# A two-network kernel after linear attention: the first network's first chunk in two halves, with the second chunk between them

## The chip, the cores and the metric

The kernel runs on one core of one Trainium2 chip. The metric is the device time of one execution, in microseconds (us). The core has five engines, each with a queue of its own that runs in order: TensorE (PE in the profile; its weight loads are PEld), VectorE (DVE), ScalarE (ACT), GpSimd (POOL) and SyncE (SP, used here for DMA issues). Sixteen DMA engines move data between DRAM and the on-chip memory SBUF; TensorE writes to PSUM, eight banks of 128 x 512 fp32.

## The reference

```python
def _attn_ref(q, k, v, alpha):            # 4 x 8 heads, 768 steps, head size 48
    for t in range(S):
        state = alpha[:, :, t, :, None] * state + np.einsum('bhd,bhe->bhde', k[:, :, t], v[:, :, t])
        y[:, :, t] = np.einsum('bhd,bhde->bhe', q[:, :, t], state)
def _moe_ref(x, w_in, w_out):             # 3072 tokens, 384 -> 2048 -> 384
    h = x @ w_in
    g = np.where(h > 0.0, h, np.exp(np.minimum(h, 0.0)) - 1.0)
    return g @ w_out
def _moe2_ref(x, domain_probs, w1, w2):   # 4 experts, 384 -> 1024 -> 384
    p = domain_probs / (domain_probs.sum(-1, keepdims=True) + 1e-09)
    for e in range(E):
        out += p[:, e:e + 1] * (np.maximum(x @ w1[e], 0.0) @ w2[e])
```

The output is the second network applied to the first network applied to the attention, for all 3072 tokens.

## The kernel before

The 768 steps are cut into six chunks of 128 (`NCH`). One chunk of all four batches is 4 x 128 = 512 tokens, the free size of every large matmul. A unit is one chunk of one batch; 24 units of attention run in order, and the state of a batch is carried from chunk to chunk.

The first network works chunk by chunk. Its 2048 hidden features are 16 slices of 128 (`F1`). For each slice `first` multiplies the chunk's input with the slice's part of w_in (`g1`, nine matmuls: three blocks of 128 inputs, and three products each because every fp32 number is split into a high and a low part), takes the ELU (`elu`: two operations on ScalarE, one on VectorE, and the split, one on each) and `second` multiplies with the slice's part of w_out (`g2a`, nine matmuls), which adds up over the slices in three PSUM banks t0, t1 and t2 (`self.xa`). The list `items` holds all pairs of chunk and slice, 96 of them; `second` runs `LA` = 2 items behind `first`. After a chunk's last slice `end1` copies the three banks to a staging tile ("stg", two buffers) on ScalarE and writes it to DRAM (`x1d`), where the second network picks it up.

The weights of the first network come as float64. `load_f64` brings one slice into a staging tile, `conv_f64` makes fp32 of it and splits it: two ScalarE and four VectorE operations (lines 71 to 78 and 327 to 328). Slice 0 is converted ahead of the loop, slice 1 is under way, and the others follow one an item, a few items ahead of their use in chunk 0. From then on all slices stay in SBUF.

The attention of chunk c + 1 runs between the items of chunk c. `unit_steps` gives six steps a unit: scores and transposes (`scores`, `ktrans`), three steps of preparation of the next unit (`prep0`, `prep1`, `prep2`), outputs and state (`yout_t`, `state`), and `xtrans`, which splits the unit's output into the chunk's input `x0`, a tile with the tag X0 or X1 by turns (`c % 2`). `yout_t` copies the output from PSUM into the one buffer "y", writes it to DRAM (`x0d`, two issues on ScalarE's queue), and reads it back in the layout that the network needs (tile `xr`, in the same buffer "y"). `slots` spreads the 24 steps of a chunk evenly over the 28 half-items of the first 14 slices (a half-item lies behind `first` or behind `second`); after every sixth step a unit of raw attention input is loaded.

`post` holds further work by item: the conversions, the preparation of the second network's weights (`prep_w`, items 20 to 91), and in the last chunk the inputs of the second network (`prep_x0`, from item 80 on). The second network follows from some 558 us on; its tiles reuse X0 and X1 (inputs' sums `xs` and weights `wa` in X0, hidden values `g` in X1).

Within the loop over the items no order is written out by hand. A planner, part of the framework, gives each engine its order when the program is built: what comes earlier in the program goes first, as soon as the planner's own costs say that its inputs and its buffer are there. On the chip each engine then keeps that order and waits where an input is late.

## Time and profile before

| | us |
|---|---|
| median of three runs | 1294.45 |
| lowest and highest | 1293.82, 1300.0 |
| the profiled execution | 1298.41 |
| its span, first to last instruction | 1296.6 |
| TensorE busy in the span | 1252.3 (97%) |
| VectorE busy | 876.4 (68%) |
| ScalarE busy | 579.5 (45%) |
| GpSimd busy | 518.5 (40%) |

The span falls into the attention of chunk 0 (0 to 42.6 us), the six chunks of the first network (first matmul of each at 42.6, 135.5, 219.3, 305.7, 391.7 and 471.9 us) and the second network, whose first matmuls begin among the last of chunk 5 at some 551 us. A busy share is a mean over stages: TensorE's 97% says that little of the whole is lost, and it is a view by stage that says where.

### The profile page before, as it was taken

To read this page: it belongs to the slowest core of one execution; us is meant where nothing else is said; L and a number is where in the kernel's file an instruction comes from. 1 tells how busy PE (TensorE), PEld (TensorE's weight loads), DVE (VectorE), ACT (ScalarE), POOL (GpSimd) and SP (SyncE) were. 2 spreads that over 40 slices of the span, in tenths; PEclk is the share of its full clock that TensorE was granted. 3 is DMA by queue.
4 is the path that set the end of the run, shared out by engine and by line. 5 is a ranking of instruction groups with operands and counts; after the bars stand their busy time and mean duration, and the time that the engine had idled before them with its cause. 6 is when DMAs were issued, how large, how long until landed. Compare 5 with 4: busy or idle time off the path is not lost.

```text
span 1296.6 us, 17731 instructions
## 1 busy us (share of the span) xinstructions
PE 1252.3 (97%) x6457; PEld 1013.4 (78%) x6457; DVE 876.4 (68%) x1510; ACT 579.5 (45%) x1076; POOL 518.5 (40%) x405
## 2 busy tenths in 40 slices
PE   8999999999999987999999999899999999999997
PEld 6776787877777876878878888788888878888886
DVE  8899977786877632366756666566767576757664
ACT  5666756665666645434333242334332333233241
POOL 0000000000000046068777564887956465456562
PEclk8999999999999998999999999999999999999999
DMA  6545266766575631525747358765644574435232
GB/s 243 199 167 183 103 233 211 253 204 226 214 255 178 227 105 50 218 89 216 254 153 270 109 190 321 273 234 200 245 184 163 211 294 171 173 105 205 98 114 72
DMA packets 71535, 246.70 MB, mean 190 GB/s; under 512 B 6680, under 2 KB 38264, under 8 KB 62096
## 3 DMA queue, kind: packets, MB, share of 16 engines
q1 hardware_dynamic: 68016, 236.84, 51.4%
q10 hardware_dynamic: 3424, 8.65, 1.7%
q8 instruction: 53, 0.87, 0.3%
q14 instruction: 42, 0.34, 0.1%
HBM read 182.11 MB, written 63.36 MB: 189 GB/s over the span
## 4 chain that ended last, share of the span: by engine, by line
PE 68%; DMA 10%; DVE 10%; POOL 4%; ACT 4%; issue 3%; SPq 1%; ACTq 0%; DVEq 0%; POOLq 0%
PE h L648 22%; PE t L698 13%; PE a L698 9%; PE h L366 7%; PE t L389 7%; PE h L698 4%; DMA x0d<-yt 3%; DMA raw<-in_att_dram 2%; DMA wraw<-in_we_dram 2%; DMA xr<-x0d 1%; DVE wh L328 1%; DVE u L668 1%; DVE h L379 1%; DVE g L328 1%; PE a L267 1%
## 5 line engine op out<-in xcount | busy, mean ns | idle before, releaser
L668 DVE TENSOR_TENSOR u<-h,u 128x512 f32<-128x512 f32 x258 | 177.4, 688 | 89.1 <-PE h L648 87.9
L389 PE MATMUL t<-g,w_W 128*128 128x512 f32 x864 | 220.3, 396 | 16.0 <-ACT x1raw L850 10.8
L366 PE MATMUL h<-x,w_W 128*128 128x512 f32 x864 | 218.5, 395 | 7.8 <-DVE g L328 5.6
L648 PE MATMUL h<-xc_Q,wa 128*128 128x512 f32 x780 | 219.3, 391 | 3.5 <-DVE c L668 2.4
L628 POOL TENSOR_TENSOR g_W<-c,g_W 128x512 fp32r<-128x512 f32 x128 | 164.4, 1299 | 122.0 <-ACT c L627 103.8
L389 PEld LDWEIGHTS t<-g,w_W 128*128 128x128 f32 x864 | 161.4, 189 | 53.9 <-ACT x1raw L850 11.2
L626 ACT ACTIVATE g_W<-c 128x512 fp32r<-128x512 f32 x128 | 80.0, 626 | 272.2 <-DVE c L668 158.8
L493 POOL TENSOR_TENSOR xs<-xr 128x512 f32<-128x512 f32 x8 | 10.1, 1274 | 471.0 <-DMA xr<-x1d 471.0
L366 PEld LDWEIGHTS h<-x,w_W 128*128 128x128 f32 x864 | 160.3, 189 | 45.6 <-DVE g L328 7.3
L648 PEld LDWEIGHTS h<-xc_Q,wa 128*128 128x128 f32 x780 | 145.7, 188 | 36.5 <-DVE c L668 3.7
L698 PE MATMUL t<-g_W,wb 128*128 128x512 f32 x576 | 157.6, 389 | 0.0
L698 PEld LDWEIGHTS t<-g_W,wb 128*128 128x128 f32 x576 | 108.1, 188 | 22.6 <-POOL g_W L628 0.2
L627 ACT ACTIVATE c<-c 128x512 f32<-128x512 f32 x192 | 121.0, 632 | 7.4
L668 DVE TENSOR_TENSOR c<-u,h 128x512 f32<-128x512 f32 x123 | 84.0, 685 | 50.2 <-PE h L648 37.8
L648 PE MATMUL h<-xc_W,wa 128*128 128x512 f32 x390 | 110.2, 391 | 4.6 <-DVE u L668 2.6
L662 DVE COPY u<-h 128x512 f32<-128x512 f32 x99 | 68.1, 690 | 66.8 <-PE h L648 66.5
L698 PE MATMUL a<-g_W,wb 128*128 128x512 f32 x384 | 111.8, 390 | 0.6 <-POOL g_W L628 0.6
L628 POOL TENSOR_TENSOR g_X<-c,g_X 128x512 fp32r<-128x512 f32 x64 | 82.7, 1304 | 62.6 <-ACT c L627 51.7
L379 DVE SCALAR_TENSOR_TENSOR h<-e,h 128x512 f32<-128x512 f32 x96 | 66.3, 690 | 56.4 <-ACT e L378 56.2
L626 ACT ACTIVATE g_X<-c 128x512 fp32r<-128x512 f32 x64 | 40.0, 626 | 141.7 <-DVE c L668 78.5
L648 PEld LDWEIGHTS h<-xc_W,wa 128*128 128x128 f32 x390 | 72.7, 188 | 22.2 <-DVE u L668 4.0
L328 DVE TENSOR_TENSOR g<-h,g 128x512 fp32r<-128x512 f32 x96 | 65.9, 687 | 30.5 <-ACT g L327 30.2
(138 smaller groups left out, 1935.7 us busy)
## 6 DMA issues: line engine op xcount, KB each, us to landing
wa<-wad SPq DMA_DIRECT2D x33, 1536.0 KB, 6.7
wb<-wbd SPq DMA_DIRECT2D x30, 1536.0 KB, 6.6
raw<-in_att_dram SPq DMA_DIRECT2D x22, 960.0 KB, 6.4
wad<-wh SPq DMA_DIRECT2D x44, 384.0 KB, 2.5
wbd<-wh SPq DMA_DIRECT2D x43, 384.0 KB, 3.3
xcd<-xh SPq DMA_DIRECT2D x30, 512.0 KB, 3.0
wraw<-in_wm_dram SPq DMA_DIRECT2D x16, 768.0 KB, 4.3
wraw<-in_we_dram SPq DMA_DIRECT2D x20, 576.0 KB, 5.4
```

Of the source, the lines that this page charges most:

```text
L267: nc.tensor.matmul(ps[64 * j:64 * j + 64, a * C:(a + 1) * C], self.st[b][r, a, :], raw[r, Q0 + a * C:Q0 + (a + 1) * C], start=(a == 0), st ...
L328: (eng or nc.vector).tensor_tensor(out=lo, in0=src, in1=hi.bitcast(F32), op=ALU.subtract)
L366: nc.tensor.matmul(h[:, 0:n], w[:, wl, fi, k * 128:(k + 1) * 128], x[:, xl, k, n0:n0 + n], start=(k == 0 and i == 0), stop=(k == KD - 1 an ...
L379: nc.vector.scalar_tensor_tensor(out=h, in0=e, scalar=-1.0, in1=h, op0=ALU.add, op1=ALU.max)
L389: nc.tensor.matmul(self.xa[k][:, 0:n], w[:, wl, fi, DM + k * 128:DM + (k + 1) * 128], g[:, gl, 0:n], start=(f == 0 and i == 0), stop=(f == ...
L626: nc.scalar.activation(out=g[:, n, 0], in_=v, func=AF.Relu)
L627: nc.scalar.activation(out=v, in_=v, func=AF.Relu)
L628: nc.gpsimd.tensor_tensor(out=g[:, n, 1], in0=v, in1=g[:, n, 0].bitcast(F32), op=ALU.subtract)
L648: nc.tensor.matmul(b, w[:, wl], x[:, xl], start=(j == 0), stop=(j == 2))
L662: nc.vector.tensor_copy(out, b)
L668: (nc.vector if "b" in (a0, a1) or dst == "S5" else nc.gpsimd).tensor_tensor(out=out, in0=val(a0, b), in1=val(a1, b), op=ALU.add if op == ...
L698: nc.tensor.matmul(oa[m, d], wt[:, f, wl, d * 128:(d + 1) * 128], G[m][:, f, gl], start=first, stop=last)
```

## The change

The list of items gets a new order: chunk 0's slices 0 to 7, chunk 1's 16 slices, chunk 0's slices 8 to 15, and then chunks 2 to 5 as before. At the end of chunk 0's first half the three banks are copied out as at the end of a chunk and written to a new DRAM tile `x1p`; they are read back into a staging tile at item 28, and at the end of the second half VectorE adds them to the banks, in place of ScalarE's copies.

Chunk 1's attention then has its 24 steps in the twelve half-items of the first six items. Chunk 2's attention has one step in each of items 19 to 23 and the rest in items 23 to 29, since its input uses the tag X1, which chunk 1 reads until item 23. The conversions of slices 8 and 9 stand at items 6 and 8, those of slices 10 to 15 at items 12 to 17, two items behind their loads; slices 3 to 7 stay where they were. The tags of the inputs follow the new order (`XTAG`), and in the second network X0 and X1 change places. The computation is the same but for the order in which the two halves of chunk 0's sums are added.

```diff
--- before.py
+++ after.py
@@ -25,6 +25,8 @@
 Q0, K0, A0, V0 = 0, NP * C, 2 * NP * C, 3 * NP * C
 UW = V0 + DM
 LA = 2
+FS = 8
+XTAG = (0, 1, 1, 0, 1, 0)
 SW = 64 + D
 REBASE = 2.0 ** -112
 P_LO, P_SUM = 1e-16, 1e15
@@ -88,6 +90,7 @@
         self.ok = ok
         self.att, self.wm, self.we, self.probs, self.out = att, wm, we, probs, out
         self.x0d = [dram.tile([2 * D, NP * C], F32, name=f"x0d{b}") for b in range(B)]
+        self.x1p = dram.tile([128, KD, 512], F32, name="x1p")
         self.x1d = [dram.tile([128, KD, 512], F32, name=f"x1d{c}") for c in range(NCH)]
         self.wad = [dram.tile([128, 12, 2, 128], F32, name=f"wad{g}") for g in range(NG)]
         self.wbd = [dram.tile([128, 3072], F32, name=f"wbd{g}") for g in range(NG)]
@@ -311,7 +314,7 @@
         c, b = u
         y = self.y.pop(u)
         if c not in self.x0:
-            self.x0[c] = self.big.tile([128, 2, KD, 512], F32R, tag=f"X{c % 2}", name=f"x0_{c % 2}")
+            self.x0[c] = self.big.tile([128, 2, KD, 512], F32R, tag=f"X{XTAG[c]}", name=f"x0_{XTAG[c]}")
         x0 = self.x0[c]
         if c:
             v = y
@@ -380,15 +383,15 @@
         self.split(g[:, 0, 0:n], g[:, 1, 0:n], h)
         return g
 
-    def g2a(self, w, fi, g, n, f):
-        nc = self.nc
-        if f == 0:
+    def g2a(self, w, fi, g, n, first, last):
+        nc = self.nc
+        if first:
             self.xa = [self.bank(f"t{k}") for k in range(KD)]
         for k in range(KD):
             for i, (wl, gl) in enumerate(((0, 0), (0, 1), (1, 0))):
                 nc.tensor.matmul(
                     self.xa[k][:, 0:n], w[:, wl, fi, DM + k * 128:DM + (k + 1) * 128], g[:, gl, 0:n],
-                    start=(f == 0 and i == 0), stop=(f == F1 - 1 and i == 2),
+                    start=(first and i == 0), stop=(last and i == 2),
                 )
 
 
@@ -507,7 +510,7 @@
                     )
                 x[m, k] = t
 
-        tmp = self.big.tile([128, 6, 512], F32, tag="X0", name="xs")
+        tmp = self.big.tile([128, 6, 512], F32, tag="X1", name="xs")
         sn, v = [0], {}
 
         def base(p):
@@ -596,7 +599,7 @@
         self.xc.setdefault(r, []).append(t)
 
     def load_wa(self, i):
-        t = self.big.tile([128, 12, 2, 128], F32R, tag=("W2", "X0")[i % 2], name="wa")
+        t = self.big.tile([128, 12, 2, 128], F32R, tag=("W2", "X1")[i % 2], name="wa")
         self.nc.sync.dma_start(out=t.bitcast(F32), in_=self.wad[i % NG])
         self.wa[i] = t
 
@@ -650,7 +653,7 @@
                 if isinstance(dst, tuple):
                     m, f = dst
                     if m not in G:
-                        t = ("W6", "X1", "W7")[self.gn % 3]
+                        t = ("W6", "X0", "W7")[self.gn % 3]
                         self.gn += 1
                         G[m] = self.big.tile([128, 3, 2, 512], F32R, tag=t, name=f"g_{t}")
                     out = self.ctile()
@@ -793,18 +796,29 @@
         self.ab = ("a0", "a1")
         pe_order.__exit__(None, None, None)
 
-        blocks = [(c, (0, 1, 2, 3)) for c in range(NCH)]
-        per = [units[4 * c + 4:4 * c + 8] for c in range(NCH)]
-        items = [(bi, f) for bi in range(len(blocks)) for f in range(F1)]
+
+
+        parts = [(0, 0, FS), (1, 0, F1), (0, FS, F1)] + [(c, 0, F1) for c in range(2, NCH)]
+        items = [(c, f, a, b) for c, a, b in parts for f in range(a, b)]
         n1 = len(items)
+        half = lambda a, b: [(i, k) for i in range(a, b) for k in range(2)]
         slots = {}
-        for bi, us in enumerate(per):
-            steps = [s for u in us for s in seq[units.index(u)]]
-            av = [(bi * F1 + f, k) for f in range(F1 - LA) for k in range(2)]
+        for c in range(1, NCH):
+            steps = [s for u in units[4 * c:4 * c + 4] for s in seq[units.index(u)]]
+            if c == 1:
+                av = half(0, FS - LA)
+            elif c == 2:
+                av = half(F1 + FS - 1, 2 * F1 - LA)
+            else:
+                av = half(F1 * (c - 1), F1 * c - LA)
             for n, s in enumerate(steps):
-                slots.setdefault(av[n * len(av) // len(steps)], []).append(s)
+                if c == 2:
+                    k = (F1 + FS - 5 + n, 0) if n < 5 else av[(n - 5) * len(av) // (len(steps) - 5)]
+                else:
+                    k = av[n * len(av) // len(steps)]
+                slots.setdefault(k, []).append(s)
                 if n % 6 == 5:
-                    slots[av[n * len(av) // len(steps)]].append([(load_next, ())])
+                    slots[k].append([(load_next, ())])
 
         def open_p2():
             self.attn.__exit__(None, None, None)
@@ -813,10 +827,13 @@
 
         post = {}
         at = lambda i, f, *a: post.setdefault(i, []).append((f, a))
-        for f in range(nf, F1):
+        for f in range(nf, FS):
             at(f - nf, self.conv_f64, f)
+            at(f - nf, self.load_f64, f + 2)
+        for f in range(FS, F1):
+            at((FS - 2, FS)[f - FS] if f < FS + 2 else f + 2, self.conv_f64, f)
             if f + 2 < F1:
-                at(f - nf, self.load_f64, f + 2)
+                at(f + 2, self.load_f64, f + 2)
         b5 = n1 - F1
         at(b5 - 2, open_p2)
         at(F1 + 1, self.norm_probs)
@@ -838,24 +855,34 @@
         gs = {}
 
         def first(it):
-            bi, f = it
-            c, bs = blocks[bi]
-            n = 128 * len(bs)
-            h = self.g1(self.w1[f // 2], f % 2, self.x0[c], bs[0] * 128, n)
-            gs[it] = self.elu(h, n)
-
-        def end1(c):
-            t = self.stg.tile([128, KD, 512], F32, tag="stg", name="x1raw")
+            c, f = it[:2]
+            h = self.g1(self.w1[f // 2], f % 2, self.x0[c], 0, 512)
+            gs[it] = self.elu(h, 512)
+
+        part = []
+
+        def load_part():
+            t = self.stg.tile([128, KD, 512], F32, tag="stg", name="x1part")
+            nc.sync.dma_start(out=t, in_=self.x1p)
+            part.append(t)
+
+        at(2 * F1 - 4, load_part)
+
+        def end1(c, a, b):
+            t = part.pop() if a else self.stg.tile([128, KD, 512], F32, tag="stg", name="x1raw")
             for k in range(KD):
-                nc.scalar.copy(t[:, k], self.xa[k])
-            nc.scalar.dma_start(out=self.x1d[c], in_=t)
+                if a:
+                    nc.vector.tensor_tensor(out=t[:, k], in0=self.xa[k], in1=t[:, k], op=ALU.add)
+                else:
+                    nc.scalar.copy(t[:, k], self.xa[k])
+            nc.scalar.dma_start(out=self.x1d[c] if b == F1 else self.x1p, in_=t)
 
         def second(it):
             g = gs.pop(it)
-            bi, f = it
-            self.g2a(self.w1[f // 2], f % 2, g, 512, f)
-            if f == F1 - 1:
-                end1(bi)
+            c, f, a, b = it
+            self.g2a(self.w1[f // 2], f % 2, g, 512, f == a, f == b - 1)
+            if f == b - 1:
+                end1(c, a, b)
 
         for i in range(n1):
             first(items[i])
```

## Rows read from the trace of the kernel before

**Rows 1.** The page: VectorE's busy tenths in 40 slices of the span.
```profile
DVE  8899977786877632366756666566767576757664
```

**Rows 2.** Busy time by stretch: first matmul of chunks 0, 1, 2 and 3.
```profile
core 0: us, PE busy (x) PEld busy (x) DVE busy (x) ACT busy (x) POOL busy (x), PEclk, DMA share, GB/s
42.60:135.50 92.90, 86.34 (x559) 66.34 (x559) 88.64 (x145) 60.59 (x105) 0.00 (x0) 1.00 0.52 179
135.50:219.30 83.80, 82.20 (x545) 66.88 (x545) 68.62 (x153) 53.72 (x119) 0.00 (x0) 1.00 0.57 198
219.30:305.70 86.40, 83.91 (x561) 67.75 (x560) 66.18 (x144) 53.36 (x118) 0.00 (x0) 1.00 0.64 221
```

**Rows 3.** TensorE's waits, whole span: who waited for what: us, times, longest.
```profile
PE t L389 <- ACT x1raw L850: 10.8, 1, 10.8
...
PE t L389 <- ACT g L327: 2.8, 4, 1.3
...
PE h L366 <- ACT w_W L327: 2.2, 3, 1.2
```

**Rows 4.** Timeline of TensorE in chunk 1: start, length, instructions merged.
```profile
144.34 1.09 PE L267 MATMUL a<-raw,st 48*64 48x128 f32 x16
...
146.82 2.34 PE L366 MATMUL h<-x,w_W 128*128 128x512 f32 x9
149.00 2.20 PE L389 MATMUL t<-g,w_W 128*128 128x512 f32 x9
151.04 2.20 PE L366 MATMUL h<-x,w_W 128*128 128x512 f32 x9
...
155.22 1.16 PE L218 MATMUL a<-raw 48*128 48x128 f32 x16
...
156.72 2.32 PE L366 MATMUL h<-x,w_W 128*128 128x512 f32 x9
```

**Rows 5.** VectorE's groups, 42.6 to 135.5 us: count | busy us, mean ns | idle.
```profile
L328 DVE TENSOR_TENSOR w_W<-cv,w_W 128x768 fp32r<-128x768 f32 x15 | 14.3, 954 | 2.0 <-ACT w_W L327 1.9
L75 DVE SCALAR_TENSOR_TENSOR cv<-wraw,cv 128x768 int32<-128x768 int32 x14 | 13.3, 950 | 0.0
...
L379 DVE SCALAR_TENSOR_TENSOR h<-e,h 128x512 f32<-128x512 f32 x15 | 10.3, 688 | 0.7 <-ACT e L378 0.7
L328 DVE TENSOR_TENSOR g<-h,g 128x512 fp32r<-128x512 f32 x15 | 10.2, 683 | 1.4 <-ACT g L327 1.4
L72 DVE TENSOR_SCALAR cv<-cv 128x768 int32<-128x768 int32 x14 | 7.6, 546 | 0.0
L181 DVE TENSOR_TENSOR_SCAN P<-raw,plo 128x128 f32<-128x128 f32 x19 | 6.5, 402 | 0.0
L224 DVE TENSOR_TENSOR sm<-a,mask 128x512 f32<-128x512 f32 x10 | 6.5, 680 | 0.0
```

**Rows 6.** Timelines of ScalarE and VectorE: copies into "y", splits out of it.
```profile
52.65 0.57 ACT L279 COPY yt<-a 112x512 f32<-112x512 f32 x1
75.86 0.58 ACT L279 COPY yt<-a 112x512 f32<-112x512 f32 x1
...
62.60 0.54 DVE L328 TENSOR_TENSOR x<-xr,x 128x384 fp32r<-128x384 f32 x1
87.96 0.55 DVE L328 TENSOR_TENSOR x<-xr,x 128x384 fp32r<-128x384 f32 x1
```

**Rows 7.** DMA issues of the page: count, KB each, median us to landing.
```profile
x1d<-x1raw ACTq DMA_DIRECT2D x6, 768.0 KB, 3.9
```

**Rows 8.** Timeline of ScalarE and TensorE at chunk 4's end, idle before in brackets.
```profile
491.37 0.62 ACT L327 CAST xc_Q<-xs 128x512 fp32r<-128x512 f32 x1 [6.23 <-POOL xs L493]
...
493.02 4.21 PE L389 MATMUL t<-g,w_W 128*128 128x512 f32 x9 [10.76 <-ACT x1raw L850]
497.02 2.98 PE L366 MATMUL h<-x,w_W 128*128 128x512 f32 x9
499.84 2.20 PE L389 MATMUL t<-g,w_W 128*128 128x512 f32 x9
```

## The prediction

> **What bounds the kernel now.** I read three views in this order. First the page: the span is the table's 1296.6 us, and the row of tenths of VectorE shows nines only in the slices that lie between some 65 and 162 us [rows 1]. Then the busy time by stretch, cut at the first matmul of each chunk of the first network: in chunk 0's stretch, 42.6 to 135.5 us, VectorE is busy 88.64 of 92.90 us (95%), in chunk 1's 68.62 of 83.80 (82%), in chunk 2's 66.18 of 86.40 (77%) [rows 2]. So TensorE sets the pace nearly everywhere, and VectorE only in chunk 0. Then TensorE's waits there: the named ones are short; 2.8 and 2.2 us are for ScalarE's casts of the hidden layer and of the weights, all of them in that stretch, and those casts themselves follow VectorE's work [rows 3].
>
> How much chunk 0 loses: one group of nine matmuls (a slice's first or second layer) takes 2.04 us from start to start (149.00 to 151.04); a unit of attention takes TensorE 144.34 to 146.82 = 2.48 us for its outputs and state and 155.22 to 156.72 = 1.50 us for scores and transposes, and the group after each part 2.18 for 2.04, so some 4.2 us [rows 4]. The stretch of chunk 0 holds 16 first and, because the second layer runs two slices late, 14 second groups, four units and the scores of a fifth: 30 x 2.04 + 4 x 4.2 + 1.1 = 79.1 us. It took 92.9, so 13.8 us are lost. Chunk 1 by the same count needs 32 x 2.04 + 16.8 - 1.1 = 81.0 and took 83.8 (2.8 lost), chunk 2 needs 82.1 and took 86.4 (4.3 lost) [rows 2]. 13.8 us is the most that a change to chunk 0 alone can win, 1.1% of the time.
>
> Why VectorE is full there: 14 conversions of weights, each 0.950 + 0.948 (a second such operation) + 0.546 + 0.954 = 3.40 us by mean durations [rows 5], lie beside the four units and the ELUs. The groups of that view add up to 98.4 us against 88.64 busy, since each operation starts a little before the one ahead ends: what follows is multiplied by 0.90.
>
> **The change, part by part.** I call the three new parts A (chunk 0, slices 0 to 7, items 0 to 7), B (chunk 1, items 8 to 23) and C (chunk 0, slices 8 to 15, items 24 to 31); from item 32 on the order is the old one.
>
> Moved: the conversions of slices 8 to 15, 8 x 3.40 x 0.90 = 24.5 us of VectorE, go out of the first 93 us and stand beside B's 65.3 us of matmuls. B's VectorE work is then 24.5 + 16 ELUs x 1.37 x 0.90 = 19.7, and some 10 for the probabilities, the first second-network weights and the first steps of chunk 2: 54 of 65 us. I cost B at nothing; the cover is those 11 us, and if it were gone it would cost what chunk 1 loses now, 2.8.
>
> Squeezed: the four units of chunk 1 have twelve half-slices instead of 28. Two things set when item 8, which needs all four, can begin.
> VectorE: the last step of one conversion and six whole ones 21.3 us, the units 26.6 (scans 5.5, masks 5.2, four 128x512 operations a unit, at the ELU's 0.68, 10.9, splits 2.2, states 2.8), eight ELUs 11.0; together 58.9 x 0.90 = 53.0 us. Chunk 2's first preparation and the last two ELUs (6.1) are not needed for item 8. At the 95% seen now that is 49.4 to 55.8 us after 42.6: item 8 at 92.0 to 98.4 [rows 2, 5].
> The one buffer "y": a unit's output is copied into it, goes to DRAM, comes back into it and is split, and only then may the next unit's copy start. From the copy's start to the end of the split it now takes 52.65 to 63.1 = 10.5 us for the first unit and 75.86 to 88.5 = 12.6 for the slowest; four units lie between 10.4 and 12.6, 11.1 in the mean [rows 6]. The first copy can stand at 49 (an estimate: its step comes a slice sooner) to 52.65, so the fourth split ends at 94 to 97.5. I take 97.5, the later ends of both.
>
> TensorE's work that can run before item 8 is eight first and eight second groups and four units: 16 x 2.04 + 16.8 = 49.4 us, until 92.0. So a wait of 5.5 us is left in A. In TensorE's queue the last two second groups may stand behind item 8's first group (they do in the order of the program; the planner may draw them ahead): 4.1 us or nothing, I take 2. A loses 7.5 where chunk 0 lost 13.8: minus 6.3. The bounds: minus 12.8 (a wait of 1 us) and plus 4.5 (the chain at 12.6 a unit, item 8 at 103.5, 11.5 us after 92.0, both groups behind it, 4.1, and the lower clock of below, 2.7: 18.3 for 13.8).
>
> C: chunk 2's first unit waits in "y" with its split until item 23 has read chunk 1's input (both use X1); what is queued behind that split is ScalarE's ELU work of the same item, which needs the same matmuls, so nobody waits longer. Three units follow in the buffer, 3 x 11.1 = 33 us, while TensorE has 8 items and three units, 45 us: a margin of 12. VectorE in that stretch: 19 of 24 steps of the units 19, eight ELUs 9.9, weights of the second network at chunk 2's rate (66.18 less units 23.9 and ELUs 19.7, so 22.6 over 16 slices) 11.3, three additions 1.9: 42 of 45 to 47 us, 90%. That lies between chunk 1's 82% (2.8 us lost) and chunk 0's 95% (13.8 lost in twice the length): 1 to 6, less the share that this half loses now (1.4). I take plus 1.5, nearest to chunk 1's row, with bounds 0 and 4.5.
>
> Added: one more end of a part, three ScalarE copies like those that now end a chunk and one issue on ScalarE's queue; at all chunk ends but one nobody waits for such copies, the next part's first group covers them [rows 3]. It writes 768 KB, as the write of a chunk does, 3.9 us to landing [rows 7]. The sums come back by one load on SyncE's queue at item 28, five items (over 20 us) before their use, into a staging buffer that is free by then; what stands behind it in that queue is loads that are as early. Cost nothing, and 3.9 us once if it had no cover. At the end of C three VectorE additions replace three copies: a 128x512 operation on a PSUM operand is 0.69 [rows 5], the group of 2.04 us ahead of the next part covers the first, and VectorE's queue is 90% full there: 0 to 2.5 us, I take 0.5.
>
> The swap of X0 and X1 in the second network changes no dependency that I can find. The long wait at 482 to 493 us, where chunk 4's end stands in ScalarE's queue behind casts that wait for GpSimd [rows 8], lies far from the change; I leave it as it is.
>
> Sum: -6.3 + 1.5 + 0.5 = -4.3. On the profiled execution's 1298.4 that is 1294.1; that execution is 4 us above the median of the runs, 1294.45, and from the median it is **1290.1**.
>
> One row speaks against a single long wait in place of many short ones. After the wait of 10.76 us the next nine matmuls took 493.02 to 497.02 = 4.00 us, half rate, the 1.2 GHz level, and the nine after them 2.82: 2.7 us more than two groups cost [rows 8]; the many short waits of chunk 0 left the granted clock at 1.00 [rows 2]. The Trainium skill, "TensorE: Matmul & The Clock Gate", section "HAM oscillation — how this bites in real kernels", says that an idle gap that is long enough puts the array back to half rate, and that the way back up is then paid again after every such gap; the trace agrees at 482 us. By that rule the wait before item 8 would cost 2.7 more and the sum would be -1.6; without it, as put down, -4.3.
>
> **The rivals.**
> Slower: the pitch of the units. If the chain through "y" takes 14 us a unit because copy, split and masks now queue on a VectorE that is fuller still, item 8 starts at 53.1 + 4 x 14 = 109.1 (53.1 is 97.5 less 4 x 11.1), 17.1 us after TensorE has run dry; with the clock's 2.7 and the 2 of the order A loses 21.8 against 13.8, and with C the time is 1294.45 + 8 + 2 = 1304. It decides from 12.2 us a unit upward (item 8 at 101.8, a loss of 11.8, the gain eaten by A, C and the additions). For it: one of four chains took 12.6, and the scores of a unit now stand over 20 us ahead of its split. Against it: three of four took 10.4 to 11.1 on a VectorE that was 95% busy.
> Nothing won: the wait comes back whole in front of item 8, or half there and half in C; 1294 to 1297. For it: A has nearly as much VectorE work per matmul as chunk 0 had (53.0 to 49.4 us).
> More won: the planner draws all eight second groups ahead and item 8 starts by 95 us: A loses 1 to 3, and with C and the additions at 0 to 2 the time is 1281.6 to 1286; or the long wait at 482 us falls away too when the planner orders ScalarE anew, 13 us more, some 1277. Against it: both limits of A lie behind 92.0.
>
> **How the numbers follow.** The forecast (1.5 to 8 us won) 0.50, nothing won 0.17, slower 0.18, more won 0.15. Half a per cent, about what a measurement of this kernel can tell from no change, is 6.5 us: faster by more has the 0.15 and some 0.20 of the forecast's 0.50; slower by more has 0.12 of the rival's 0.18; the rest is within. The range leaves out the late wait's end and the rival's far end: 1281 to 1299.5.
>
> **What would show it.** The first group of item 8 at 95 to 100 us, with one wait of 3 to 8 us ahead of it; copies into "y" 10 to 12 us apart between 50 and 90; VectorE over 95% busy until then and under 85% in B; B's 16 items in 66 to 68 us; the start of item 32 at most 3 us late; the wait at chunk 4's end unchanged. The second network starts some 4 us sooner than 558.3 and takes as long as before. Wrong it would be if the units come 13 us or more apart, if the wait ahead of item 8 passes 10 us, or if the late wait moves.

## The result and the profile after

The changed kernel takes 1314.19 us (median of four runs, 1313.34 to 1314.4); the kernel before, run beside it, 1297.22. The ratio of the runs is 1.0124 with a 95% interval of 1.0079 to 1.0169 (the intervals below are of the same kind, each against the kernel before run beside it): some 16 us slower, where 4 us less had been forecast, and outside the range. The profiled execution of after has a span of 1312.6 us for 1296.6. Cut at the first matmul of the same items, the 16.0 us between the two spans lie here:

| stretch, by items | before, us | after, us | difference |
|---|---|---|---|
| start to item 0 | 42.6 | 40.9 | -1.7 |
| 0 to 15 (after: A and half of B) | 92.9 | 95.0 | +2.1 |
| 16 to 31 (after: the rest of B, then C) | 83.8 | 83.7 | -0.1 |
| 32 to 47 (chunk 2) | 86.4 | 92.3 | +5.9 |
| 48 to 63 (chunk 3) | 86.0 | 88.5 | +2.5 |
| 64 to 79 (chunk 4) | 80.2 | 81.2 | +1.0 |
| 80 to the second network (chunk 5) | 78.9 | 82.3 | +3.4 |
| second network | 745.8 | 748.7 | +2.9 |

The gain that was forecast for the first row of items is a small loss, and most of the loss lies behind item 32, where the order of the items is the old one. From the page of after, VectorE's tenths, a digit for 32.8 us:

```profile
span 1312.6 us, 17739 instructions
DVE  8889978777777742366756665566667575757664
```

Two nines for the three of before [rows 1], and they lie from 98 to 164 us, nearly all in B: in A, where VectorE was to be fuller than ever, stand eights. The busy times by stretch say it in numbers: A, B and C alone, then the stretches of 16 items that answer to [rows 2]. Columns: the stretch and its length, busy time with instructions of PE, PEld, DVE, ACT and POOL, the granted clock, the DMA share, GB/s.

```profile
40.90:104.50 63.60, 57.26 (x418) 43.18 (x417) 55.19 (x96) 38.15 (x70) 0.00 (x0) 0.95 0.55 187
104.50:174.00 69.50, 69.47 (x357) 56.78 (x358) 60.62 (x107) 46.49 (x86) 0.00 (x0) 1.00 0.38 127
174.00:219.60 45.60, 44.62 (x329) 35.91 (x327) 36.27 (x79) 28.17 (x63) 0.00 (x0) 1.00 0.73 258
...
40.90:135.90 95.00, 88.62 (x556) 68.85 (x555) 84.65 (x144) 62.86 (x115) 0.00 (x0) 0.96 0.50 168
135.90:219.60 83.70, 82.72 (x549) 67.02 (x547) 67.43 (x138) 49.95 (x103) 0.00 (x0) 1.00 0.57 198
219.60:311.90 92.30, 86.15 (x560) 69.04 (x561) 68.66 (x150) 53.97 (x117) 0.00 (x0) 0.98 0.62 213
```

In A VectorE's work is 55.19 us, 2 more than the sum of the prediction, but it takes 63.6 us to do it: 87% busy, not 95. In B TensorE is busy 69.47 of 69.50 us and waits for nobody, as forecast; the 69.5 us are over the 66 to 68 that were named as a sign, and VectorE's 60.62 us (87%) over the 54 and the 85%. Why A is slow stands in these lines of the timeline of after, from the split of its first unit to the copy of its third:

```profile
58.82 0.56 DVE L331 TENSOR_TENSOR x<-xr,x 128x384 fp32r<-128x384 f32 x1 [1.85 <-ACT x L330]
59.91 1.28 DVE L227 TENSOR_TENSOR sm<-a,mask 128x512 f32<-128x512 f32 x2
65.53 0.59 ACT L282 COPY yt<-a 112x512 f32<-112x512 f32 x1 [0.31 <-PE a L277]
77.15 0.56 DVE L331 TENSOR_TENSOR x<-xr,x 128x384 fp32r<-128x384 f32 x1 [1.37 <-ACT x L330]
78.22 0.68 DVE L227 TENSOR_TENSOR sm<-a,mask 128x512 f32<-128x512 f32 x1
79.94 0.96 PE L277 MATMUL a<-sm,raw 128*48 128x128 f32 x13
81.05 0.59 ACT L282 COPY yt<-a 112x512 f32<-112x512 f32 x1 [2.06 <-PE a L277]
```

Read it as one chain. VectorE's queue is in order, and in it the mask of the next unit's scores stands directly behind the split of this one (both masks behind the first split, the second of two behind the second). The split waits for the round trip of "y" through DRAM, VectorE idles for it (1.85, 1.37 us), and only then come the mask, TensorE's outputs of the next unit and their copy into "y". So the parts that [rows 6] show far apart in the kernel before are in series: copy to the end of the split takes 9.9, 12.2, 10.5 and 10.7 us, in the prediction's bounds of 10.4 to 12.6 or just below, but from the end of a split to the next copy pass another 6.1, 3.4 and 2.8. (In the 6.1 TensorE ran at half rate, as shown below: the unit's two groups of 16 matmuls took 1.97 and 1.95 us, in the fourth unit 1.09 and 1.08.) The copies stand at 49.47, 65.53, 81.05 and 94.43, 15.0 us apart in the mean. Item 8 starts at 104.5, and the loss does not stand ahead of it as one wait. Two of TensorE's waits in A, at 59 and 87 us, and the one at item 8:

```profile
59.33 0.77 PE L392 MATMUL t<-g,w_W 128*128 128x512 f32 x2 [1.97 <-ACT g L330]
...
87.68 0.66 PE L238 MATMUL h<-ident,raw 128*128 128x128 f32 x4 [1.96 <-DVE raw L203]
...
104.53 0.73 PE L369 MATMUL h<-x,w_W 128*128 128x512 f32 x2 [0.49 <-ACT x L330]
```

The clock fell too. Granted clock (0.50 is the 1.2 GHz level) in two stretches of after, the first of them right behind the wait at 59 us, and then around the wait at 87 us:

```profile
59.90:66.70 6.80, 6.80 (x53) 5.46 (x53) 6.56 (x13) 4.21 (x9) 0.00 (x0) 0.50 0.03 14
247.60:251.00 3.40, 3.40 (x10) 2.66 (x9) 2.85 (x6) 2.70 (x7) 0.00 (x0) 0.50 0.97 335
```

```profile
84.00:92.00 8.00, 5.90 (x35) 3.60 (x33) 8.00 (x16) 7.08 (x13) 0.00 (x0) 1.00 0.67 244
```

A third such stretch of 3.4 us lies at 582 us, behind a wait of 2.17 us. None of the three is in the trace of before. TensorE is busy all through them, so they cost at most half of 13.6 us, 6.8 of the 16; in the first, VectorE is busy 6.56 of the 6.80 us too, so what it cost is not shown. The wait of 1.96 us at 87.68 left the clock at 1.00: the length of the single wait does not decide.

In chunk 2's stretch the loss is in the first eight items (50.1 us where before took 43.2; the other eight are 1.0 shorter). Its largest wait, in the timeline of after:

```profile
234.26 0.95 SPq L174 DMA_DIRECT2D raw<-in_att_dram  x1
...
243.67 0.42 DVE L184 TENSOR_TENSOR_SCAN P<-raw,plo 128x128 f32<-128x128 f32 x1 [3.11 <-DMA raw<-in_att_dram]
...
246.48 0.68 DVE L331 TENSOR_TENSOR g<-h,g 128x512 fp32r<-128x512 f32 x1
247.21 3.04 PE L369 MATMUL h<-x,w_W 128*128 128x512 f32 x7 [3.72 <-DVE g L331]
```

A load of a unit's input lands 9.4 us after its issue; VectorE stands 3.11 us at the scan that needs it; an ELU's split stands behind that scan, and TensorE waits 3.72 us for the split. Last, the long wait at chunk 4's end, beside [rows 8]:

```profile
505.58 0.62 ACT L330 CAST xc_Q<-xs 128x512 fp32r<-128x512 f32 x1 [6.23 <-POOL xs L496]
507.23 3.80 PE L392 MATMUL t<-g,w_W 128*128 128x512 f32 x9 [12.82 <-ACT x1raw L877]
```

It is 12.82 us for 10.76: the cast still waits the same 6.23 us for GpSimd, and the copies stand later behind it.

### The profile page after: what moved, and what is told of

It reads as the page before. It is cut to its first block, busy times and chain, and to the rows that moved or that the text cites. A ratio compares the mean times of both kernels' runs of the same rounds, so it can differ in the third digit from the quotient of the medians.

```text
span 1312.6 us, 17739 instructions
## 1 busy us (share of the span) xinstructions
PE 1256.6 (96%) x6457; PEld 1015.8 (77%) x6457; DVE 880.5 (67%) x1513; ACT 580.4 (44%) x1076; POOL 517.8 (39%) x405
## 3 DMA queue, kind: packets, MB, share of 16 engines
q1 hardware_dynamic: 68160, 237.62, 51.1%
## 4 chain that ended last, share of the span: by engine, by line
PE 64%; DMA 13%; DVE 11%; POOL 4%; ACT 4%; issue 2%; SPq 1%; ACTq 0%; DVEq 0%; POOLq 0%
PE h L651 22%; PE t L701 13%; PE a L701 9%; PE h L369 6%; PE t L392 6%; PE h L701 4%; DMA wraw<-in_we_dram 4%; DMA raw<-in_att_dram 4%; DMA x0d<-yt 2%; DVE u L671 2%; DMA xr<-x0d 2%; DVE wh L331 1%; DVE wc L420 1%; DVE h L382 1%; DVE P L184 1%
## 5 line engine op out<-in xcount | busy, mean ns | idle before, releaser
L671 DVE TENSOR_TENSOR u<-h,u 128x512 f32<-128x512 f32 x258 | 177.6, 688 | 89.8 <-PE h L651 88.7
L496 POOL TENSOR_TENSOR xs<-xr 128x512 f32<-128x512 f32 x8 | 10.2, 1289 | 485.3 <-DMA xr<-x1d 485.3
L369 PEld LDWEIGHTS h<-x,w_W 128*128 128x128 f32 x864 | 161.1, 190 | 51.6 <-DVE g L331 12.6
L701 PEld LDWEIGHTS a<-g_W,wb 128*128 128x128 f32 x384 | 72.6, 189 | 16.3 <-POOL g_W L631 1.1
```

The lines of the kernel that those rows point to most:

```text
L369: nc.tensor.matmul(h[:, 0:n], w[:, wl, fi, k * 128:(k + 1) * 128], x[:, xl, k, n0:n0 + n], start=(k == 0 and i == 0), stop=(k == KD - 1 an ...
L671: (nc.vector if "b" in (a0, a1) or dst == "S5" else nc.gpsimd).tensor_tensor(out=out, in0=val(a0, b), in1=val(a1, b), op=ALU.add if op == ...
L701: nc.tensor.matmul(oa[m, d], wt[:, f, wl, d * 128:(d + 1) * 128], G[m][:, f, gl], start=first, stop=last)
```

## The experiments

**Is it the one buffer "y"?** The changed kernel with two such buffers (the same for the three tiles that use it):

```
-        y = self.ap.tile([128, NP * C], F32, tag="y", name="yt")
+        y = self.ap.tile([128, NP * C], F32, tag="y", name="yt", bufs=2)
```

> The changed kernel with two buffers "y" instead of one, so that a unit's output may be copied out while the unit ahead is still on its way through DRAM. Theory 1 (the one buffer sets the pitch of chunk 1's units, 15 us instead of the 11.1 that I took): the copies come 10 to 12 us apart, item 8 starts at 92 to 97 us instead of 104.5, and the time falls by 7 to 12 us. Theory 2 (VectorE's queue in part A sets it, and the copy waits for masks and preparations that stand late in that queue): the pitch stays at 13 to 16 us, item 8 stays within 2 us of 104.5, and the time changes by less than 3 us.

1311.84 us, 1.0121 of before (1.0067 to 1.0175). Item 8 starts at 102.2 from an item 0 at 37.2, so A takes 65.0 us for the 63.6 without; the copies are still 15.6 us apart. Lines of its timeline, second to third unit:

```profile
61.73 0.58 ACT L282 COPY yt<-a 112x512 f32<-112x512 f32 x1
73.33 0.56 DVE L331 TENSOR_TENSOR x<-xr,x 128x384 fp32r<-128x384 f32 x1 [2.82 <-ACT x L330]
74.41 0.68 DVE L227 TENSOR_TENSOR sm<-a,mask 128x512 f32<-128x512 f32 x1
78.78 0.58 ACT L282 COPY yt<-a 112x512 f32<-112x512 f32 x1 [3.61 <-PE a L277]
```

The buffer is free and the copy still comes after the split, because the mask of its unit does. The buffer is not the cause; VectorE's order is.

**Units prepared further ahead.** The changed kernel, and the one before, with four buffers for a unit's input (and two for "P", to make room). It takes away the wait for the load at 243 us:

```
-        t = self.ap.tile([128, UW], F32, tag="raw", name="raw", bufs=3)
+        t = self.ap.tile([128, UW], F32, tag="raw", name="raw", bufs=4)
...
-        P = self.ap.tile([128, NP, C], F32, tag="P", name="P", bufs=3)
+        P = self.ap.tile([128, NP, C], F32, tag="P", name="P", bufs=2)
```

> The changed kernel with four buffers for a unit's raw input instead of three (and two instead of three for the running products P, which makes the room). Theory 4 (behind item 32 the time goes where VectorE's in-order queue stands at the scan of a unit's preparation, drawn ahead by the planner, until the unit's raw input has landed, and the ELUs stand behind it: 3.1 us at 243.7 us in the changed kernel, TensorE waits 3.7): with the load a unit earlier these waits go, chunk 2's stretch falls from 92.3 us to 85 to 88, chunk 3's from 88.4 to 85 to 87, and the time falls by 5 to 10 us. Theory 5 (ScalarE's casts of the second network's weights, which wait for their own load, hold the ELUs): the stretches stay within 2 us and so does the time.

> The kernel before with the same four raw buffers and two for P. Theory 4: VectorE's waits for raw inputs, 11 us in all over the chunks and at most 1.8 at a time, go, and since TensorE lost little by them the time falls by 1 to 4 us. Theory 5: no difference beyond 2 us. If the running products' third buffer mattered, chunk 0's stretch grows above 94 us.

In the changed kernel 1309.89 us, 1.0098 (1.0065 to 1.0131); in the one before 1308.35, 1.0068 (1.0039 to 1.0097), slower than without; item 0 starts at 51.1 us there, for 42.6. The windows of the changed kernel's run, A first, then chunk 2's stretch:

```profile
54.50:102.70 48.20, 47.23 (x399) 37.78 (x399) 46.54 (x86) 31.12 (x61) 0.00 (x0) 1.00 0.57 197
...
224.40:315.40 91.00, 85.87 (x562) 68.80 (x561) 71.32 (x159) 54.56 (x121) 0.00 (x0) 0.98 0.63 220
```

Two things follow. With more prepared ahead, the masks stand ahead of the splits, and the chain is what the prediction had sized; lines of the timeline of the same run:

```profile
66.65 1.26 DVE L227 TENSOR_TENSOR sm<-a,mask 128x512 f32<-128x512 f32 x2
73.39 0.56 DVE L331 TENSOR_TENSOR x<-xr,x 128x384 fp32r<-128x384 f32 x1
74.36 0.58 ACT L282 COPY yt<-a 112x512 f32<-112x512 f32 x1
```

Copies at 63.27, 74.36, 84.41, 93.32: 10.0 us apart; VectorE 97% busy, A 48.2 us long. But the work that was drawn ahead has only moved: item 0 starts at 54.5 and item 8 at 102.7, as late as in the changed kernel. VectorE has 89.34 us of work until then (88.61 in the changed kernel); even at this 97% all the way from the start they take until 92. And chunk 2's stretch, with no VectorE wait for a load left in it, is still 91.0, not the 85 to 88 of theory 4: that wait is where the loss shows, not why it is there.

**Each half of the exchange alone.** The kernel before, with chunk 1's attention squeezed into six items and nothing else changed:

```
-            av = [(bi * F1 + f, k) for f in range(F1 - LA) for k in range(2)]
+            av = [(bi * F1 + f, k) for f in range(6 if bi == 0 else F1 - LA) for k in range(2)]
```

> The kernel before with one part of the change alone: chunk 1's attention in the first six items instead of the first 14. The order of the chunks and the conversions stay. VectorE's work in chunk 0 is the same in sum, so if VectorE's sum sets chunk 0's stretch it stays at 92 to 95 us with the waits moved to its first half, and the later chunks stay within 2 us of before. If squeezed units cost by themselves (their chains and the raw loads bunched): the stretch grows above 96, or the next chunk's does by over 3.

The kernel before, with the weights of slices 8 to 15 neither loaded nor converted:

```
-        for f in range(nf, F1):
+        for f in range(nf, F1 // 2):
             at(f - nf, self.conv_f64, f)
...
+        def same():
+            for j in range(F1 // 4, F1 // 2):
+                self.w1[j] = self.w1[j - F1 // 4]
...
```

> The kernel before without the loads and conversions of the weights of slices 8 to 15, in whose place the weights of slices 0 to 7 are used again. It measures what moving those conversions could win at most. If VectorE's conversions are what chunk 0 loses by: its stretch falls from 92.9 us to 80 to 83, and the time falls by 10 to 13 us. If the units of attention are what it loses by: the stretch stays above 88 us and less than 5 us are won.

Squeezed: 1307.23 us, 1.0066 (1.0041 to 1.0091). Without the conversions: 1314.5, 1.0141 (1.009 to 1.0192). Chunk 0's stretch in the first:

```profile
41.00:144.80 103.80, 95.20 (x591) 70.66 (x591) 92.90 (x152) 63.53 (x112) 0.00 (x0) 0.95 0.48 165
```

and chunk 0's and 1's in the second:

```profile
41.00:125.00 84.00, 82.41 (x544) 65.62 (x544) 71.23 (x126) 53.37 (x102) 0.00 (x0) 1.00 0.37 128
125.00:213.70 88.70, 84.91 (x562) 68.81 (x561) 64.38 (x141) 51.01 (x109) 0.00 (x0) 0.98 0.58 199
```

In the first the copies into "y" stand 15.6 us apart, as in the changed kernel, and in the stretch TensorE ran 10.2 us at half rate. The squeeze costs 10.9 us there (103.8 for 92.9), of which chunk 1's stretch gives back 2.2 (81.6 for 83.8); the conversions taken away, with their loads, win 8.9. So there is a gain to be had from the conversions, and the squeeze that the change needs for it costs about as much. That 10.9 less 8.9 comes near the 2.1 of the changed kernel is chance, though: there 11 conversions still lie in items 0 to 15 (14 before), since those of slices 8 to 13 only moved to items 6 to 15. The second run also shows how little a win in chunk 0 is worth by itself here: chunk 1 gives back 4.9 us, chunk 5 6.2 and the second network 10.5, in an order that was drawn anew. One wait of 7.1 us for TensorE's own issue at 550 us and one of 3.7 for a load of weights are named there; the rest was not traced.

**Half of the split to GpSimd**, which is idle in that stretch: the kernel before, subtraction for slices 3 to 15.

```
-        self.split(w[:, 0, f % 2], w[:, 1, f % 2], tf)
+        self.split(w[:, 0, f % 2], w[:, 1, f % 2], tf, nc.gpsimd if f > 2 else None)
```

> The kernel before with the subtraction in the weights' conversion (0.95 us of VectorE each) on GpSimd, which is idle until 471 us, for slices 3 to 15. It takes 13 x 0.87 = 11.3 us of VectorE out of chunk 0 and moves nothing. If VectorE's sum sets chunk 0's stretch (as the run without conversions says): the stretch falls from 92.9 us to 82 to 86 and the time by 5 to 9 us. If the gain is given back in the later stretches, as there: less than 3 us.

1310.83 us, 1.0084 (1.006 to 1.0107). Chunk 0's stretch is 99.4 us, 6.5 longer. GpSimd's group, the waits of TensorE, the stretch, one of VectorE's groups in it, and two of its operations in the timeline beside GpSimd's:

```profile
L328 POOL TENSOR_TENSOR w_W<-cv,w_W 128x768 fp32r<-128x768 f32 x13 | 26.9, 2073 | 107.9 <-ACT w_W L327 107.9
```

```profile
PE h L366 <- POOL w_W L328: 7.7, 7, 2.7
```

```profile
41.00:140.40 99.40, 87.12 (x543) 67.12 (x544) 94.21 (x137) 63.62 (x112) 26.95 (x13) 0.97 0.48 167
```

```profile
L75 DVE SCALAR_TENSOR_TENSOR cv<-wraw,cv 128x768 int32<-128x768 int32 x14 | 18.7, 1335 | 0.0
```

```profile
62.54 2.10 POOL L328 TENSOR_TENSOR w_W<-cv,w_W 128x768 fp32r<-128x768 f32 x1 [5.72 <-ACT w_W L327]
63.48 1.97 DVE L75 SCALAR_TENSOR_TENSOR cv<-wraw,cv 128x768 int32<-128x768 int32 x1
...
69.46 1.81 POOL L328 TENSOR_TENSOR w_W<-cv,w_W 128x768 fp32r<-128x768 f32 x1 [4.82 <-ACT w_W L327]
69.77 2.32 DVE L75 SCALAR_TENSOR_TENSOR cv<-wraw,cv 128x768 int32<-128x768 int32 x1
```

2.07 us on GpSimd for 0.95 on VectorE [rows 5]: the weight is ready later, and TensorE waits for it seven times. And VectorE was not relieved. Thirteen subtractions of 0.95 us are gone from it, yet it is busy 94.21 us where it was busy 88.64 [rows 2]: some of its operations that begin while GpSimd subtracts last until shortly after GpSimd has ended (65.45 behind 64.64, 72.09 behind 71.27), and this group's mean is 1.34 us for 0.95. The run therefore does not say what a VectorE with less work would win.

**Why chunk 2's stretch is longer.** First suspect: the preparation of the second network's weights, which runs there. The changed kernel with that preparation given to later items:

```
-WPREP = (20, 92)
+WPREP = (34, 92)
```

> The changed kernel with the preparation of the second network's weights spread over items 34 to 91 instead of 20 to 91, so that none of it runs in part C or at its end. Theory 3 (the loss behind item 32 comes from that preparation: it falls behind on a full VectorE in part C, its writes hold up SyncE's queue, and the raw inputs of chunk 3's units are loaded late): chunk 2's stretch, 92.3 us in the changed kernel and 86.4 before, falls to 86 to 88, and the time falls by 3 to 6 us although the later chunks get a quarter more of that work per item. Rival (the squeezed units themselves, or the planner's order of them, lose the time): chunk 2's stretch stays at 91 to 93.

> The changed kernel with the second network's weights prepared in items 48 to 91 only, so that chunk 2's stretch (items 32 to 47) has none of their loads, casts and writes. Theory 5: chunk 2's stretch falls to 83 to 86 us, about the work on TensorE alone. Theory 4: the scans still wait for raw inputs, whose loads then have the DMA engines to themselves, and the stretch is 87 to 90. In both the later chunks get two thirds more of that work per item, so chunks 3 and 4 grow by 2 us or more each.

1317.91 us, 1.0167 (1.0116 to 1.0219), and with 48 in place of 34 1314.84, 1.0125 (1.0074 to 1.0176). Neither run decides between the theories: VectorE still does 18 of these steps in items 16 to 31 and 27 in 32 to 47 in all three kernels. The planner draws them ahead, so the item number does not place them, and the edit does not do what it says. The runs show something else. With none of these steps moved out of it, the stretch of items 16 to 31 takes 88.8 and 88.7 us where the changed kernel took 83.7, and in the kernel before an edit behind item 80 (prep_x0 on VectorE, below) has it at 86.7 for 83.8. So a stretch differs by up to 5 us from kernel to kernel, through a planner's order drawn anew or from one execution to another (one trace each cannot tell which), and a difference of that size in one stretch does not show what an edit costs.

So the preparation was left out, but for one group in eleven, in both kernels (the second network's loads then all read that group):

```
-        wsteps = [s for g in range(NG) for s in self.prep_w(g)]
+        wsteps = self.prep_w(0)
```

> The changed kernel with one group in eleven of the second network's weights prepared; the second network reads that group eleven times (the other ten groups' preparation is left out). Theory 8 (the stalls behind item 32 come from the preparation's casts and writes, which stand in the in-order queues waiting for their loads, and which the item numbers do not place: the planner draws them ahead): chunks 1 to 4, 345.6 us together in the changed kernel, fall by 12 us or more, chunk 2's stretch to 82 to 85. Rival (raw inputs and the way through DRAM of the units): chunk 2's stretch stays above 88.

> The kernel before with the same ten groups of preparation left out, as the other side of the comparison. Theory 8: chunks 1 to 4, 336.4 us together, fall by 6 to 12 us, so that the difference between the two kernels behind item 32 is gone (under 2 us). Rival: the two differ by 5 us or more behind item 32, as with the preparation.

1294.39 us (1290.21 to 1297.53) for the changed kernel, 1291.63 (1287.1 to 1295.76) for the one before. Chunk 2's stretch in the changed kernel and in the one before:

```profile
218.00:301.00 83.00, 83.00 (x562) 67.92 (x561) 48.50 (x89) 40.66 (x81) 0.00 (x0) 1.00 0.23 77
```

```profile
213.20:296.30 83.10, 83.10 (x561) 67.83 (x561) 45.76 (x84) 41.93 (x82) 0.00 (x0) 1.00 0.24 77
```

83.0 and 83.1; chunk 3 82.9 and 83.0; chunk 4 79.6 in both. Without the preparation the change costs nothing in chunks 2 to 4 (chunk 5 and the second network are 1.3 and 1.0 us longer, chunks 0 and 1 2.4 each). The loss there, 9.4 us, needs two partners: the changed order and the work that fills VectorE, ScalarE and the DMA queues around it.

Which part of the change? The kernel before, with chunk 2's attention alone placed as in the changed kernel (five steps at items 19 to 23, the rest in items 23 to 29):

```
+            if bi == 1:
+                av = [(f, k) for f in range(23, 30) for k in range(2)]
...
+                if bi == 1:
+                    k = (19 + n, 0) if n < 5 else av[(n - 5) * len(av) // (len(steps) - 5)]
...
```

> The kernel before with chunk 2's attention placed as in the changed kernel: a step in each of items 19 to 23, the rest in items 23 to 29, instead of all spread over items 16 to 29. Nothing else is changed. Theory 6 (a squeezed chunk of attention costs by itself, in its own stretch or just behind it, as chunk 1's did with 10.8 us): chunk 1's and chunk 2's stretches together, 170.2 us in the kernel before and 176.0 in the changed one, come to 174 to 178. Theory 7 (the loss behind item 32 comes from the second half of chunk 0 and its additions): they stay at 169 to 172.

1306.17 us, 1.0055 (1.0036 to 1.0074). Chunk 1's stretch, then chunk 2's:

```profile
134.00:220.60 86.60, 83.51 (x545) 68.41 (x544) 66.82 (x150) 53.31 (x116) 0.00 (x0) 0.98 0.55 189
220.60:315.70 95.10, 88.46 (x562) 70.87 (x561) 69.63 (x151) 56.13 (x123) 0.00 (x0) 0.95 0.59 204
```

Plus 2.8 in the stretch that is squeezed and plus 8.7 in the one behind it, where not one step of that squeeze stands by its item number; chunks 3 to 5 together are 1.9 shorter. The second stretch holds 10.2 us at half rate, around TensorE's waits of 3.86 and 2.28 us; TensorE is busy 9.5 of them, so they cost at most 4.7 of the 8.7. VectorE waits there up to 4.9 us for a unit's raw input. In the order that was drawn here the squeeze of chunk 2 is enough for the loss in chunk 2's stretch, and most of its price falls behind it.

The other part that reaches item 32 is the kept sums. The changed kernel without their load and additions, so that the sums of slices 0 to 7 of chunk 0 are missing from its output:

```
-        at(2 * F1 - 4, load_part)
...
-            t = part.pop() if a else self.stg.tile([128, KD, 512], F32, tag="stg", name="x1raw")
+            t = self.stg.tile([128, KD, 512], F32, tag="stg", name="x1raw")
...
-                if a:
-                    nc.vector.tensor_tensor(out=t[:, k], in0=self.xa[k], in1=t[:, k], op=ALU.add)
-                else:
-                    nc.scalar.copy(t[:, k], self.xa[k])
+                nc.scalar.copy(t[:, k], self.xa[k])
```

> The changed kernel without the use of the kept sums: no load of the first half's sums, no additions on VectorE, at the end of chunk 0's second half ScalarE copies the banks as at any other end (so the first half's sums are left out of the result). Theory 7: chunk 2's stretch falls from 92.3 to 86 to 88 us and the time by 4 to 7. Theory 6: chunk 2's stretch stays at 90 to 93 and the time within 2 us, which would put the price of keeping the sums in DRAM at nothing, as I had it.

1310.41 us, 1.0093 (1.0074 to 1.0111). Chunk 2's stretch:

```profile
219.80:307.60 87.80, 84.91 (x561) 67.87 (x562) 67.44 (x147) 55.97 (x121) 0.00 (x0) 1.00 0.65 226
```

4.5 us shorter than in the changed kernel, at the full clock (3.4 us at half rate are gone, at most 1.7 of the 4.5). If it is the sums, keeping them costs some 4 us and not 0.5. That is not shown clear of the noise: the ratio's interval overlaps that of the changed kernel (1.0079 to 1.0169), 4.5 us in one stretch is no more than the 5 us above, and chunk 0's stretch, which lies before what was left out, is 2.7 longer in this run (97.7 for 95.0). The two prices of that stretch, 8.7 for the squeeze in the kernel before and 4.5 for the sums in the changed one, do not add up to its 5.9: each was taken in another order of the whole. How they share it is open.

**The long wait at chunk 4's end.** The kernel before, with that chunk's end copies on VectorE:

```
-                nc.scalar.copy(t[:, k], self.xa[k])
+                if c == NCH - 2:
+                    nc.vector.tensor_copy(t[:, k], self.xa[k])
+                else:
+                    nc.scalar.copy(t[:, k], self.xa[k])
```

> The kernel before with the three copies at chunk 4's end on VectorE instead of ScalarE, where they stand behind casts that wait for GpSimd. If that place in the queue is the whole cause of the wait of 10.8 us at 482 us: it goes, with the stretch at half rate behind it, and the time falls by 10 to 14 us, to some 1282. If TensorE would wait there for something else too (the ELUs stand in the same queue behind the same casts): less than 5 us are won.

1300.74 us, 1.0022 (0.9992 to 1.0053): no difference. From its waits of TensorE:

```profile
PE t L389 <- DVE x1raw L851: 8.8, 2, 5.0
```

The wait is cut in two. VectorE stands in its turn, once for 6.14 us, behind ELU results that come from the same queue of casts. The copies were the last link, not the cause. The suspect is GpSimd's pace, which ScalarE's order hands on. So the sums and splits of the second network's first inputs were taken from GpSimd and given to VectorE, in both kernels (the calls for the sums, likewise, take VectorE in place of GpSimd):

```
-            self.split(t[:, i, 0], t[:, i, 1], y, nc.gpsimd)
+            self.split(t[:, i, 0], t[:, i, 1], y)
```

> The kernel before with the sums and splits of the second network's first inputs (prep_x0) on VectorE, which is busy 27.5 of 86.4 us in chunk 5's stretch, instead of GpSimd. ScalarE's casts then wait 0.7 us for each instead of 1.3, and fewer of them stand ahead of chunk 4's copies. Theory 9 (the long wait at chunk 4's end is the pace of GpSimd in ScalarE's order): the wait of 10.8 us falls below 3, the half rate behind it goes, and the time falls by 9 to 13 us. Rival (what is won in the first network is given back where the second begins, as in the run without conversions): less than 4 us.

> The changed kernel with the same move of prep_x0 to VectorE. It tells whether the 3.3 us that chunk 5's stretch and the 2.9 us that the second network are longer in the changed kernel hang on the long wait (12.8 us there). Theory 9: the wait goes and more is won than in the kernel before, 11 to 15 us, and the two kernels then differ by 10 to 13 us. Rival: the difference of 16 us stays within 2.

The kernel before becomes 1286.46 us, 0.9888 (0.9856 to 0.992): faster than both kernels of the case. The changed one becomes 1298.07, 0.9983 (0.9959 to 1.0008). Chunk 5's stretch, in the one before and in the changed one:

```profile
473.80:539.10 65.30, 65.30 (x289) 54.08 (x288) 37.79 (x60) 37.77 (x66) 0.00 (x0) 1.00 0.39 138
```

```profile
477.70:543.70 66.00, 65.72 (x290) 53.92 (x289) 37.98 (x60) 37.38 (x66) 0.00 (x0) 1.00 0.41 148
```

65.3 us for 78.9, and 66.0 for 82.3: the wait is gone in both, so GpSimd's pace was its cause, and of the 3.4 us of chunk 5 all but 0.7 came with it. Without it the changed kernel is still 11.6 us behind by the medians. (The profiled execution of the changed one, with a span of 1289.0 us, was the shortest of its ten, 1290.77 to 1301.58. Only the stretch above is read from it.)

Last, this gain together with GpSimd's half of the conversions, in the kernel before:

> Both moves in the kernel before: prep_x0 on VectorE and the conversions' subtraction on GpSimd. If both gains hold and add: 1277 to 1284 us where the kernel before has 1299. If either is given back behind it: the better of the two runs alone.

1297.62 us, 0.9984 (0.9955 to 1.0013). Chunk 0's stretch is 100.7, chunk 5's 65.3: the loss of the one and the gain of the other, side by side; neither of the two outcomes that were expected came.

## Why the prediction was wrong

**What bounds the kernel** held: TensorE nearly everywhere, VectorE in chunk 0. The lost 13.8 us are there to be won in part: without the conversions of slices 8 to 15 and their loads the stretch is 84.0.

**A, minus 6.3: wrong, and the first step that failed.** The term was taken as "the later ends of both" of two limits, VectorE's sum and the chain through "y", as if they ran side by side. In VectorE's queue they are one chain, since masks stand behind splits that wait. VectorE's work was sized well (55.19 us for 53.0) and the chain from copy to split too (10.8 in the mean for 11.1); what was not counted is the way from a split to the next copy, 4.1 us in the mean, VectorE's own waits (87% busy for 95%), and the 6.8 us at half rate in A. The stretch of 16 items came out 2.1 longer, 8.4 us off the term. The wait was placed wrong as well: 5.5 us ahead of item 8 in the sum, 0.49 there in the trace. (52.65 and four chains of 11.1 make 97.05, not 97.5; that slip decides nothing.) Two of the three signs that were to mean wrong came: units over 13 us apart, and a late wait that moved.

The chain was not the only limit. In the run with four raw buffers the pitch is 10.0 us and item 8 starts only 1.8 us sooner, since item 0 starts 13.6 us later: what was gained behind it had been spent ahead of it.

The rival "Slower: the pitch of the units" named the mechanism, with its point of decision at 12.2 us; the pitch was 15.0. Its reason was partly right, since masks queue on VectorE, but the buffer was not what held them: two buffers left the pitch at 15.6. It had a chance of 0.18 because three of four chains took 10.4 to 11.1; those rows were of a kernel in which units lie 23 us apart [rows 6], where the next unit's mask has long room behind a split. Its arithmetic counted four pitches; three pitches and one chain from the first copy (49.47 + 45.0 + 10.7) give the end of the last split at 105.1.

**B, nothing:** the cost was right, TensorE waits for nobody; that its 16 items take 66 to 68 us was not, they took 69.5.

**C, plus 1.5: wrong place.** C alone took 45.6 us, and the stretch that it ends is as before (83.7), within the bounds of 0 to 4.5. But it was priced by that stretch alone, and its cost lies in the one behind: 8.7 us more there when the squeeze is made alone in the kernel before, and a part that is open of the 5.9 in the changed one. The step "weights of the second network at chunk 2's rate" saw that filler and took it as work that adds up; the pair without the preparation shows that without it there is no loss in chunks 2 to 4.

**Additions, 0.5:** probably mis-sized, some 4 us where its bound was 2.5, but not shown clear of the noise. It was priced as a write, a load and three operations, each with a cover.

**The late wait, unchanged:** it grew from 10.76 to 12.82, with chunk 5's stretch 3.4 longer. That it is tied to GpSimd's pace [rows 8] was right, as prep_x0 on VectorE shows. Whether the exchange of X0 and X1 has a part in the 2 us was not tried.

**The clock.** The row that the prediction put aside weighed more than its 2.7 us. The lower level did come back: after 1.97 us at 59.33 and after 3.72 at 247.21 TensorE ran at half rate for 6.8 and 3.4 us, while chunk 0 of before, with no single wait above 1.42 us, kept its clock at 1.00 [rows 2]. The Trainium skill, "TensorE: Matmul & The Clock Gate", section "HAM oscillation — how this bites in real kernels", has it that the way back up is paid after each long gap; the trace agrees after 3.72 us, and leaves open what a long gap is, with half rate behind 1.97 us and none behind 1.96.

**All that lies behind item 32, nothing but the additions' 0.5: wrong, and the larger step.** Chunk 0's 13.8 us were taken as the arena, and the rest of the kernel as unmoved, because "from item 32 on the order is the old one". That holds for the items and not for the planner's order on the engines. Of the 16.0 us between the spans 15.7 lie behind item 32; that is 15.2 of the 20.3 us by which the forecast missed, where A is 8.4 (the start and C came out 3.3 better). Open are: what of chunks 3 and 4 (3.5 us, gone without the preparation) goes to which part; and the second network's 2.9. It took 745 to 751 us in all kernels here but one, whatever was changed, so that may be no effect of the change at all.

## What to carry to other kernels

A dependent chain that is squeezed on an in-order queue costs the sum of its links as that queue orders them, not the later of two limits: look what stands behind each waiting instruction. Run the two halves of an exchange (work moved away, work squeezed) alone before they are run together. Work given to an idle engine need not relieve the full one: look at the full engine's busy time afterwards. A price can fall in the stretch behind, where filler work is drawn ahead; price a stretch together with the filler, and mistrust a few microseconds in one stretch when an edit elsewhere moves it as much. And the largest single wait in the trace is the first thing to try: here 10.8 us, and moving the operations that it came from off the slow engine won 1.1% of the kernel before.

## What the runs showed of the hardware

A subtraction of 128x768 fp32 with two inputs took 2.07 us on GpSimd and 0.95 on VectorE, a ratio of 2.2. The Trainium skill, "GPSIMD Engine Reference", section "4.1 Engine selection", puts such operations at about twice VectorE's time; the trace agrees. Two VectorE operations that began during such a subtraction took 1.97 and 2.32 us for 0.95, and ended 0.8 us after it. A load of a unit's input took 9.4 us to its use, with a load of weights issued 0.5 us ahead of it and the write of a chunk's sums 1.6 us behind; one in the kernel before, with the same neighbours 3.6 us ahead and 2.6 us behind, took 6.6. That the neighbours make the difference is not shown. And the clock fell to its lower level behind a wait of 1.97 us, and not behind one of 1.96 us, 28 us later in the same part.
